# Attention slots one step later, two splits earlier, and two sets of decayed keys on GpSimd

## The chip, the cores and the metric

The kernel runs on one core of one Trainium2 chip. The metric is the device time of one execution in microseconds (us). The engines are TensorE (PE; its weight loads are shown apart as PEld), VectorE (DVE), ScalarE (ACT), GpSimd (POOL) and SyncE (SP, which here only issues DMAs).

## The reference, cut to what matters

Retention attention with a decay `lam` for each of 8 heads (2 batches, 768 positions, 64 columns a head) gives x, 1536 tokens by 512. Then two layers follow:

```python
# attention, block by block of the sequence
intra = (q k^T * Dmask) v ; inter = (q * lam_pow) kv_state
kv_state = lam_block * kv_state + (k * rev_pow)^T v      # "decayed keys" k * rev_pow
x   = attention as [1536, 512]
r   = np.maximum(x @ w_in, 0.0); x = (r * r) @ w_out     # layer 1, 512 -> 2048 -> 512
out = (1 / (1 + np.exp(-(x @ w_gate))) * (x @ w_val)) @ w_out   # layer 2, 512 -> 1536 -> 512
```

## The kernel before, in words

Everything is FP32 in value, computed on PE from two parts: each operand is split into a high part (`whi`, `xh`, `gh`) and a low part (`wlo`, `xl`, `gl`), and a product takes three groups of matmuls. A unit of layer 1's weights arrives over SP's queue as `raw` (512 KB). ACT takes it apart in two instructions (`scale_words`: `j`, `r`), DVE joins these (`join_words`: a shift and an add), the joined words are stored to DRAM (`w<-j`, 256 KB for a unit) and split: `whi` on ACT (on DVE for the first units), `wlo` on DVE, which needs `whi`. The stores free the buffers that later `j` and `r` reuse: `unit` hands out 27 buffers of 128x512 in turn, `double` 27 of 128x1024.

**Attention.** Twelve chunks of 128 positions are worked on in six pairs, (0, 6) to (5, 11). The first two pairs stand at the start. The other four are interleaved with layer 1's first block of 512 tokens ("block 0"). For a pair k there are two *scores* slots (`att_scores` on PE, a mask on DVE, a decayed query `qd` on POOL by `query`, decayed keys `kd` by `att_keys`) and one *out* slot (`att_uv`, `att_out` on PE, then the state on POOL and DVE). The table `SLOTS` says at which half step each stands, `LOADS` at which half step its q/k and k/v chunks and two pairs of weight units are asked for. `att_keys` of chunks 2 and 8 runs on ACT, eight instructions of 128x64; all others are one instruction of 128x512 on POOL.

**Block 0.** `step_1(f)` runs for f = 0 to 15; its half steps are 2f and 2f + 1. In order: A(f) (`stage_a`, through `mm_in`, 12 matmuls of a weight unit with x0 into one bank), the slot of half step 2f, `elem` and `split_g` on A(f)'s result (ACT `r`, `g`, `gh`, DVE `gl`), B(f-1) (`stage_b`, `mm_out`, 12 matmuls), the slot of half step 2f + 1, and then what `PLAN[f]` lists: `A` takes the next couple of raw units apart (`couple_act`, two ACT instructions a unit), joins them on DVE and asks for the next loads; `S` splits the oldest joined couple (`couple_split`). An `S` that leads the list is done ahead of B(f-1). The instructions stand on every engine in the order in which this program writes them; an engine works through them in that order.

**After block 0** the other 1024 tokens pass layer 1 by Strassen products (`block`, L733). Their operands are prepared at places of a clock that counts the planned matmul time (`at`, `passed`): `combine_x(1, places)` makes 11 combined operands `xch`/`xcl` (L616, L619) and differences `t` (L632), `combine_a` the weights' sums `as`, `ah`, `al`. `T1` is the planned time at which the Strassen products begin. `snap` (L742) and `evacuate` (L583) copy PSUM banks out on ACT, which frees them.

Of the kernel before, what the change touches and what calls it, by code (L numbers as in the profile page):

```python
# [9 lines left out]
AF = mybir.ActivationFunctionType  # L10
# [6 lines left out]
FILL = 8  # L17
SINGLE = 10
BY_DVE = 7
KEYS_BY_ACT = (2, 8)  # L20
PLAN = {
    0: "ASAS", 1: "ASAS", 2: "AAS", 3: "SAA", 4: "SAS", 5: "SAA", 7: "SAA", 9: "SAA",
    10: "SAS", 11: "SS", 12: "S", 13: "", 14: "", 15: "",
}

PAIRS = ((0, 6), (1, 7), (2, 8), (3, 9), (4, 10), (5, 11))
LEAD = 2
SLOTS = {
    7: ("scores", 2), 8: ("scores", 8), 10: ("out", 2),
    11: ("scores", 3), 12: ("scores", 9), 14: ("out", 3),  # L30
    15: ("scores", 4), 16: ("scores", 10), 18: ("out", 4),
    19: ("scores", 5), 20: ("scores", 11), 22: ("out", 5),
}
LOADS = {
# [3 lines left out]
}  # L38

MM = 0.2267  # L40
# [5 lines left out]
def retention_moe_kernel(  # L46
# [24 lines left out]
    nc = tc.nc  # L71
    NCH = qk.shape[0]
    NT = out.shape[2]
    SEQ_CH = NCH // 2
    H = lam.shape[0]
# [38 lines left out]
    qk_t, kv_t = {}, {}  # L114
# [143 lines left out]
    def run(ops):  # L258
        weave(ops, [])
# [4 lines left out]
    W = const.tile([P, H, 1], F32, name="W")  # L264
# [98 lines left out]
    def heads(t):  # L363
        return t.rearrange("s (h d) -> s h d", h=H)
# [11 lines left out]
    def query(i, eng=nc.gpsimd):  # L376
        b = slice(0, 64 if i == NCH else P)
        qd = qd_t[i] = unit("qd")
        eng.tensor_tensor(
            out=pv(qd)[b], in0=pv(qk_t[i][:, 0, :])[b], in1=L[b, i // (SEQ_CH + 1)],  # L380
            op=ALU.mult,
        )

    def att_keys(c, eng=nc.gpsimd):
        if c % SEQ_CH < SEQ_CH - 1:
            kd = kd_t[c] = unit("kd")
            if c in KEYS_BY_ACT:
                for h in range(H):
                    nc.scalar.activation(
                        heads(kd)[:, h], heads(kv_t[c][:, 0, :])[:, h], AF.Copy, scale=W[:, h]  # L390
                    )
                return
            eng.tensor_tensor(
                out=heads(kd), in0=heads(kv_t[c][:, 0, :]), in1=W.to_broadcast([P, H, 64]),
                op=ALU.mult,
            )

    def att_mask(c):
        s = c // SEQ_CH
        sc = sc_t.pop(c)  # L400
        at_t[c] = double("at")
        return [
            lambda g=g: nc.vector.tensor_tensor(
                out=pv(at_t[c][:, g, :]), in0=pv(sc[g]), in1=D[:, g ^ s], op=ALU.mult
            )
            for g in range(2)
        ]
# [108 lines left out]
            split_t[ph, f, u] = (hi, lo)  # L516
        return ops

    def mm_in(acc, w):
        (wh, wl), (xh, xl) = w, x0  # L520
        i = 0
        for a, b in ((wh, xh), (wl, xh), (wh, xl)):
            for kk in range(4):
                nc.tensor.matmul(  # L524
                    acc, lhsT=a[:, kk * P : (kk + 1) * P], rhs=b[:, kk, :],
                    start=i == 0, stop=i == 11,
                )
                i += 1
        passed(12 * MM)
# [14 lines left out]
    def stage_a(ph, f):  # L544
        accs = []
        for u in range(ph):
            accs.append(bank())
            mm_in(accs[u], split_t.pop((ph, f, u)))
        return accs

    def elem(ph, f, acc):
# [596 lines left out]
    def attend(half):  # L1148
        load(LOADS.get(half, ""))
        what, k = SLOTS.get(half, (None, 0))  # L1150
        if what == "scores":
            att_scores(k)
            passed(SCORES)

            def after():
                run(att_mask(k))
                att_keys(k)
                query(k if k < SEQ_CH else k + 1)
                qk_t.pop(k)

            return after
        if what == "out":
            pair = PAIRS[k]
            if k < SEQ_CH - 1:
                decayed()
            att_uv(pair)
            att_out(pair)
            for c in pair:
                kv_t.pop(c)
            passed(REST)  # L1170

            def after():
                att_state()
                att_x(pair)

            return after
        return lambda: None
# [57 lines left out]
    with tc.manual_schedule():  # L1235
        load_lam()
        load("q6", nc.scalar)
        load("q0 q7 v0 v6 w q1 q8 v1 v7 w w w w w")
        rows = decays()
        warm_up(WARM)  # L1240
        new_xr()
        first, second = PAIRS[:LEAD]
        for c in first:
            att_scores(c)
        warm_up(FILL)
        query(7)
        for c in first:
            att_keys(c)
        run([op for c in first for op in att_mask(c)])
        rows()  # L1250
        att_out(first)
        att_uv(first)
        j_0, r_0 = couple_ops()
        j_0()
        x_1 = att_x(first, r_0)
        run(couple_dve())
        att_state()
        for c in (1, 8):
            query(c)
        for c in second:  # L1260
            att_scores(c)
        lo_0 = couple_split()
        run([op for c in second for op in att_mask(c)])
        run(lo_0)
        run(x_1)
        for c in second:
            att_keys(c)
        decay_of_state()
        decayed()
        att_out(second)  # L1270
        run(att_x(second))
        for _ in range(2):
            couple_act()
            run(couple_dve())
            run(couple_split())
        att_uv(second)
        for c in (0, 6, 1, 7):
            qk_t.pop(c)
        for c in (0, 6, 1, 7):
            kv_t.pop(c)  # L1280
        clock[0] = 0.0
        flush()


        keys = [(1, i, 0) for i in range(NF1 // 2)]
        prepare_a(keys[0], T1 - 20.0)
        at(T1 - 20.0, lambda: load_a((1, 1, 0)))
        combine_x(1, [T1 + d for d in (-24, -22.5, -20.5, -18.5, -16, -13.5, -11, -8.5, -6, -3.5, -1)])
        for f in range(NF1):
            step_1(f)  # L1290
        n_out = 24
        for k in range(3):
            at(T2 - 14.0 + k, lambda: load_w(1))
        for k in range(n_out):
            convert(T2 + 1.0 + k * (T3 - T2 - 4.0) / n_out)
        for f in range(NF1):
            prepare_out(1, f, T2 + 24 * MM * f)
        uses = [use for i in range(NF1 // 2) for use in pair_in_1(i)]
        strassen(keys, uses, (None, lambda: close(1)))
        xc.clear()  # L1300
        new_xr()
        for f in range(2):
            at(T3 - 24.0 + f, lambda f=f: load_units(2, f))
        at(T3 - 14.0, lambda: run(split_w(2, 0)))
        pair_out(1)


        for f in range(2, NF2):
            at(T3 + (36 * (f - 1) - 12) * MM - 8.0, lambda f=f: load_units(2, f))
        for k in range(3 * NF2 - n_out):  # L1310
            convert(T3 + 2.0 + 3.6 * k)
        for i in range(NF2 // 2):
            sum_out_w(i, T4 - 64.0 + 9.0 * i)
        keys = [(2, i, u) for i in range(NF2 // 2) for u in range(2)]
        prepare_a(keys[0], T4)
        at(T4 - 28.0, lambda: combine_a((2, 0, 1)))
        at(T4 - 20.0, lambda: load_a((2, 0, 1)))
        combine_x(2, [T4 - 46.0 + 3.5 * k for k in range(11)])
        for f in range(NF2):
            step_2(f)  # L1320
        T6 = T5 + 6 * STEP
        by_unit_through_dram(1, T5 - 14.0, T5 - 7.0)
        through_dram(2, T5 - 4.0, T5 + 1.5)
        through_dram(3, T5 + 1.0, T5 + 6.5)
        through_dram(4, T5 + 6.0, T5 + 11.5)
        for n, load, pos in (
            (0, -21.0, -13.0), (1, -12.0, -1.5), (2, -6.0, 4.0),
            (3, 1.0, 8.8), (4, 6.0, 13.5), (5, 11.0, 18.3),
        ):
            prepare_w(0, n, n, T5 + load, T5 + pos)  # L1330
        for n, i, load, pos in (
            (0, 5, -12.5, -5.0), (1, 4, -7.5, -1.0), (2, 3, -3.0, 3.5),
            (3, 0, 1.0, 8.0), (4, 2, 6.0, 10.0), (5, 1, 10.0, 11.6),
        ):
            prepare_w(1, n, i, T6 + load, T6 + pos)
        by_unit_through_dram(2, T6 - 7.0, T6 + 5.0)
        by_unit_through_dram(1, T6, T6 + 10.2)
        uses = [use for i in range(NF2 // 2) for use in pair_in_2(i)]
        strassen(keys, uses, (None, lambda: close(2)))
        blocks_out()  # L1340
        flush()
        assert not agenda and not to_conv and not ready
# [62 lines left out]
```

## Time and profile before

| | |
|---|---|
| runs | 580.08, 581.56, 581.89 us; median 581.56 |
| profiled execution | 582.65 us, of it a span of 580.9 us that the trace shows |
| TensorE's granted clock over the span | 0.997 of 2.4 GHz |
| busy | PE 98%, DVE 77%, ACT 60%, POOL 10% |
| DMA | 150.25 MB, 259 GB/s on average |

A time in a timeline counts from the span's start. "[2.89 <-ACT whi L246]" behind a row is the idle time of that engine just before it and the work that ended it. Rows of one kind that follow each other stand as one row with their count (x4); its duration is that of the whole row.

### The profile page before, as it was taken

How to read it: one execution, taken by the hardware profiler on the slowest of the kernel's cores; microseconds unless marked ns; L12 is line 12 of the kernel's file. 1: busy time of each engine (PE TensorE's matmuls, PEld its weight loads, DVE VectorE, ACT ScalarE, POOL GpSimd, SP SyncE). 2: the span in 40 equal slices, each digit the busy share in tenths (PEclk: the TensorE clock that was granted, in tenths of full speed). 3: DMA queues.
4: the chain of work that ended last, by engine and by line, in shares of the span. 5: the costliest groups of instructions: out<-in, count | busy, mean ns of one | idle time of the engine just before them, and what ended most of it. 6: DMA issues, size and time to landing. Idle time of an engine off the chain costs nothing.

```text
span 580.9 us, 8565 instructions
## 1 busy us (share of the span) xinstructions
PE 569.4 (98%) x3018; PEld 463.4 (80%) x3018; DVE 448.1 (77%) x650; ACT 349.6 (60%) x562; POOL 55.9 (10%) x50
## 2 busy tenths in 40 slices
PE   8998999999999999999999999999999999999997
PEld 5876888888888888888888888888878888878785
DVE  7997877986788866776656778884778877779956
ACT  4678878857565557775648565534564555385452
POOL 6332351000000000000000000120102210000000
PEclk9998999999999999999999999999999999999999
DMA  8999998401454588999985899984447678588681
GB/s 309 407 408 413 343 365 292 139 18 63 129 182 151 177 313 320 410 410 412 401 335 179 292 352 343 367 254 91 139 113 207 199 198 234 166 314 312 195 321 72
DMA packets 69226, 150.25 MB, mean 259 GB/s; under 512 B 6976, under 2 KB 15168, under 8 KB 69184
## 3 DMA queue, kind: packets, MB, share of 16 engines
q1 hardware_dynamic: 65312, 144.86, 68.4%
q0 software_dynamic: 3360, 3.93, 4.5%
q10 hardware_dynamic: 512, 0.92, 0.5%
q8 instruction: 23, 0.38, 0.3%
q14 instruction: 19, 0.16, 0.1%
HBM read 105.91 MB, written 42.21 MB: 255 GB/s over the span
## 4 chain that ended last, share of the span: by engine, by line
PE 78%; DVE 7%; DMA 6%; ACT 4%; issue 2%; POOL 2%; DVEq 0%; SPq 0%; ACTq 0%; POOLq 0%
PE p L733 28%; PE p L524 17%; PE p L1124 15%; PE p L538 12%; DMA gr<-gs 2%; PE p L1053 2%; PE p L457 2%; PE p L371 1%; DMA gs<-gs 1%; DMA D<-wt 1%; DVE wq L1010 1%; DMA out_t<-c 1%; PE p L445 1%; DVE j L181 1%; DVE gs L868 1%
## 5 line engine op out<-in xcount | busy, mean ns | idle before, releaser
L733 PE MATMUL p<-xch,ah 128*128 128x512 f32 x280 | 110.0, 393 | 1.0 <-ACT s L742 0.5
L733 PE MATMUL p<-xch,al 128*128 128x512 f32 x280 | 109.1, 390 | 0.0
L733 PE MATMUL p<-xcl,ah 128*128 128x512 f32 x280 | 109.1, 390 | 0.0
L733 PEld LDWEIGHTS p<-xch,ah 128*128 128x128 f32 x280 | 52.6, 188 | 14.9 <-ACT s L742 3.2
L742 ACT COPY s<-p 128x512 f32<-128x512 f32 x60 | 35.1, 588 | 43.6 <-PE p L733 43.3
L733 PEld LDWEIGHTS p<-xch,al 128*128 128x128 f32 x280 | 52.6, 188 | 11.0
L733 PEld LDWEIGHTS p<-xcl,ah 128*128 128x128 f32 x280 | 52.6, 188 | 10.6
L747 DVE TENSOR_TENSOR c<-p,s 128x512 f32<-128x512 f32 x60 | 41.3, 688 | 23.0 <-PE p L733 23.0
L1053 PE MATMUL p<-gq,wq 128*128 128x512 f32 x252 | 58.0, 391 | 0.3 <-DVE wq L1010 0.2
L1053 PEld LDWEIGHTS p<-gq,wq 128*128 128x128 f32 x252 | 47.1, 188 | 11.1 <-DVE wq L1010 1.4
L181 DVE CUSTOM_DVE_ANT_0 j<-j,r 128x1024 uint16<-128x1024 uint16 (+1 forms) x57 | 48.5, 851 | 6.6 <-DVE j L176 0.5
L165 ACT ACTIVATE j<-raw 128x512 f32<-128x512 f32 x68 | 45.4, 668 | 10.1 <-DMA raw<-in_w 5.7
L1124 PE MATMUL p<-g2h,whi 128*128 128x512 f32 x128 | 49.8, 389 | 0.0
L1124 PE MATMUL p<-g2h,wlo 128*128 128x512 f32 x128 | 49.8, 389 | 0.0
L1124 PE MATMUL p<-g2l,whi 128*128 128x512 f32 x128 | 49.8, 389 | 0.0
L169 ACT ACTIVATE r<-raw 128x512 int32<-128x512 uint32 x68 | 45.0, 662 | 4.2 <-DMA w<-j 2.7
L524 PE MATMUL p<-xh,whi 128*128 128x512 f32 x160 | 44.5, 400 | 2.9 <-ACT whi L246 2.9
L524 PE MATMUL p<-xh,wlo 128*128 128x512 f32 x160 | 43.6, 395 | 1.3 <-DVE wlo L249 1.3
L524 PE MATMUL p<-xl,whi 128*128 128x512 f32 x160 | 42.8, 390 | 0.0
L681 POOL DMA_DIRECT2D as<-w x6 | 5.6, 926 | 354.9 <-DVE g L560 282.2
L524 PEld LDWEIGHTS p<-xh,whi 128*128 128x128 f32 x160 | 30.1, 191 | 9.8 <-ACT whi L246 3.3
L524 PEld LDWEIGHTS p<-xh,wlo 128*128 128x128 f32 x160 | 30.5, 191 | 8.3 <-DVE wlo L249 1.8
(128 smaller groups left out, 1029.0 us busy)
## 6 DMA issues: line engine op xcount, KB each, us to landing
raw<-in_w SPq DMA_DIRECT2D x68, 512.0 KB, 7.6
w<-j SPq DMA_DIRECT2D x68, 256.0 KB, 7.6
u<-w SPq DMA_DIRECT2D x52, 256.0 KB, 5.3
a<-w SPq DMA_DIRECT2D x20, 512.0 KB, 4.1
g<-g SPq DMA_DIRECT2D x32, 256.0 KB, 3.8
g<-g SPq DMA_DIRECT2D x16, 512.0 KB, 7.6
kv<-in_kv SPq DMA_DIRECT2D x12, 512.0 KB, 7.8
gr<-gs SPq DMA_DIRECT2D x24, 256.0 KB, 6.0
```

The source lines that it names most:

```text
L165: lambda: nc.scalar.activation(j, t[:, :, 1].bitcast(F32), AF.Prelu, scale=2.0**-80 if flip else 2.0**-112, alpha=2.0**-32 if flip else 2. ...
L169: lambda: nc.scalar.activation(r, low, AF.Copy, scale=2.0**-29),
L181: nc.vector.tensor_tensor(out=j, in0=j, in1=r, op=ALU.add)
L371: nc.tensor.matmul(pv(sc[g])[:, p, :], lhsT=pv(t[:, 1, :])[half(g), p, :], rhs=pv(t[:, 0, :])[half(g), p, :], start=True, stop=True,)
L457: nc.tensor.matmul(ov[s][half(r), p, :], lhsT=v[:, 2 * p + r, :], rhs=pv(at[:, r ^ s, :])[:, p, :], start=n == 0 and p == 0, stop=p == 3, ...
L524: nc.tensor.matmul(acc, lhsT=a[:, kk * P : (kk + 1) * P], rhs=b[:, kk, :], start=i == 0, stop=i == 11,)
L538: nc.tensor.matmul(acc[e], lhsT=a[:, e * P : (e + 1) * P], rhs=b, start=first and i == 0, stop=last and i == 2,)
L733: nc.tensor.matmul(acc, lhsT=w[:, col, kk * P : (kk + 1) * P], rhs=x[:, kk, :], start=start and i == 0, stop=stop and i == 5, skip_group_c ...
L742: nc.scalar.copy(s, acc)
L747: nc.vector.tensor_tensor(out=c, in0=acc, in1=s, op=ALU.add)
L1053: nc.tensor.matmul(acc[k], lhsT=a[:, wn], rhs=block_of(b, gn), start=first and n == 0, stop=last and n == 3 * len(group) - 1,)
L1124: nc.tensor.matmul(acc[e, t], lhsT=a[:, e * P : (e + 1) * P], rhs=b[:, t, :], start=first and i == 0, stop=last and i == 2,)
```

## The change

1. `SLOTS`: every slot stands two half steps, one step, later. `LOADS`: their loads one or two half steps later.
2. `PLAN`: steps 2, 3 and 4 change from `AAS`, `SAA`, `SAS` to `ASA`, `SAS`, `AAS`.
3. `KEYS_BY_ACT` is gone: the decayed keys of chunks 2 and 8 are one POOL instruction each.
4. `attend`: query and keys of a scores slot are issued directly behind its matmuls, the query first; only the mask stays behind the step's other work.
5. `mm_in` for f > 1: the group with `xl` comes second and the one with `wlo` last.
6. `combine_x(1)`: its 11 places lie between T1 - 16 and T1 - 1 instead of T1 - 24 and T1 - 1.

```diff
-KEYS_BY_ACT = (2, 8)
 PLAN = {
-    0: "ASAS", 1: "ASAS", 2: "AAS", 3: "SAA", 4: "SAS", 5: "SAA", 7: "SAA", 9: "SAA",
+    0: "ASAS", 1: "ASAS", 2: "ASA", 3: "SAS", 4: "AAS", 5: "SAA", 7: "SAA", 9: "SAA",
...
 SLOTS = {
-    7: ("scores", 2), 8: ("scores", 8), 10: ("out", 2),
...
-    19: ("scores", 5), 20: ("scores", 11), 22: ("out", 5),
+    9: ("scores", 2), 10: ("scores", 8), 12: ("out", 2),
...
+    21: ("scores", 5), 22: ("scores", 11), 24: ("out", 5),
 }
 LOADS = {
-    2: "q2", 3: "q9", 4: "v2", 5: "v8",
+    3: "q2", 4: "q9", 6: "v2", 7: "v8",
...
     def att_keys(c, eng=nc.gpsimd):
...
-            if c in KEYS_BY_ACT:
-                for h in range(H):
-                    nc.scalar.activation(
-                        heads(kd)[:, h], heads(kv_t[c][:, 0, :])[:, h], AF.Copy, scale=W[:, h]
-                    )
-                return
...
-        for a, b in ((wh, xh), (wl, xh), (wh, xl)):
+        for a, b in ((wh, xh), (wh, xl), (wl, xh)) if late else ((wh, xh), (wl, xh), (wh, xl)):
...
-                mm_in(accs[u], split_t.pop((ph, f, u)))
+                mm_in(accs[u], split_t.pop((ph, f, u)), f > 1)
...
-            def after():
-                run(att_mask(k))
-                att_keys(k)
-                query(k if k < SEQ_CH else k + 1)
-                qk_t.pop(k)
-
-            return after
+            query(k if k < SEQ_CH else k + 1)
+            att_keys(k)
+            qk_t.pop(k)
+            return lambda: run(att_mask(k))
...
-        combine_x(1, [T1 + d for d in (-24, -22.5, -20.5, -18.5, -16, -13.5, -11, -8.5, -6, -3.5, -1)])
+        combine_x(1, [T1 + d for d in (-16, -15, -13.5, -12, -10.5, -9, -7.5, -6, -4.5, -3, -1)])
```

Lines of the changed kernel stand 1 to 11 lower than before (L246 becomes L245, L524 L517, L555 L548, L619 L612, L632 L625, L697 L690, L742 L735).

ACT, from `whi` of A(5)'s weights (`whi_674`, after the change `whi_587`) to the `whi` of the couple that holds B(4)'s weights (`whi_706`, after the change `whi_669`). Before:

```order
L165 ACTIVATE j_591<-raw 128x512
L169 ACTIVATE r_592<-raw 128x512
L389 ACTIVATE kd<-kv,W 128x64 x8
L165 ACTIVATE j_613<-raw 128x512
...
L568 CAST gh<-g 128x512
L389 ACTIVATE kd<-kv,W 128x64 x8
L246 CAST whi_674<-j_591 128x512
L165 ACTIVATE j_694<-raw 128x512
...
L169 ACTIVATE r_695<-raw 128x512
L246 CAST whi_706<-j_613 128x1024
```

And after the change:

```order
L164 ACTIVATE j_579<-raw 128x512
L168 ACTIVATE r_580<-raw 128x512
L245 CAST whi_587<-j_579 128x512
L548 ACTIVATE r<-p 128x512
L549 ACTIVATE g<-r 128x512
L561 CAST gh<-g 128x512
L164 ACTIVATE j_642<-raw 128x512
...
L168 ACTIVATE r_658<-raw 128x512
L245 CAST whi_669<-j_642 128x1024
```

The row of `whi` for A(5) now follows its own `j` and `r` directly; between the two `whi` rows there are now `r`, `g`, `gh` and eight instructions that take raw units apart (`j_642`, `r_643` twice and `j_657`, `r_658` twice), where there were four (`j_694`, `r_695` twice).

POOL, behind the state of the first pairs (`tt`); the rows are those of chunks 2 and 8. Before:

```order
L411 TENSOR_TENSOR tt<-S,G 128x512
L379 TENSOR_TENSOR qd<-qk,L 128x512 x2
L411 TENSOR_TENSOR tt<-S,G 128x512
L393 TENSOR_TENSOR kd<-kv,W 128x512
L379 TENSOR_TENSOR qd<-qk,L 128x512
```

And after the change:

```order
L404 TENSOR_TENSOR tt<-S,G 128x512
L378 TENSOR_TENSOR qd<-qk,L 128x512
L386 TENSOR_TENSOR kd<-kv,W 128x512
L378 TENSOR_TENSOR qd<-qk,L 128x512
L386 TENSOR_TENSOR kd<-kv,W 128x512
L404 TENSOR_TENSOR tt<-S,G 128x512
```

Two `kd` are added there, one behind each `qd`.

DVE, the last rows ahead of the first weights' sums `as` of the Strassen part, from the `gl` of step 14 on. Before:

```order
L570 TENSOR_TENSOR gl_1546<-g_1542,gh_1545 128x512
L619 TENSOR_TENSOR xcl_1539<-t_1522,xch_1538 128x1024
L619 TENSOR_TENSOR xcl_1563<-xr_158,xch_1562 128x1024
L632 TENSOR_TENSOR t_1579<-xr_158,t_1479 128x1024
L570 TENSOR_TENSOR gl_1586<-g_1582,gh_1585 128x512
L619 TENSOR_TENSOR xcl_1602<-t_1579,xch_1601 128x1024
L697 TENSOR_TENSOR as_1617<-a_1451 128x256
```

And after the change:

```order
L563 TENSOR_TENSOR gl_1525<-g_1521,gh_1524 128x512
L625 TENSOR_TENSOR t_1540<-xr_158 128x1024
L612 TENSOR_TENSOR xcl_1514<-t_1498,xch_1513 128x1024
L612 TENSOR_TENSOR xcl_1518<-xr_158,xch_1517 128x1024
L612 TENSOR_TENSOR xcl_1545<-t_1540,xch_1544 128x1024
L625 TENSOR_TENSOR t_1564<-xr_158,t_1498 128x1024
L563 TENSOR_TENSOR gl_1571<-g_1567,gh_1570 128x512
L612 TENSOR_TENSOR xcl_1561<-xr_158,xch_1560 128x1024
L612 TENSOR_TENSOR xcl_1588<-t_1564,xch_1587 128x1024
L690 TENSOR_TENSOR as_1603<-a_1428 128x256
```

Between the `gl` of step 14 and `as` there are three rows of 128x1024 more than before: seven beside the two `gl`, where there were four.

## Rows read from the trace of the kernel before

**Rows 1.** Windows: busy time of the engines, granted clock, DMA share, GB/s.

```profile
core 0: us, PE busy (x) PEld busy (x) DVE busy (x) ACT busy (x) POOL busy (x), PEclk, DMA share, GB/s
20.00:58.00 38.00, 33.77 (x207) 26.63 (x206) 33.27 (x49) 31.25 (x63) 8.14 (x6) 0.96 1.03 410
58.00:130.00 72.00, 72.00 (x635) 58.46 (x626) 59.30 (x66) 54.96 (x85) 15.35 (x10) 1.00 0.65 232
```

**Rows 2.** Timeline of PE: start, duration (us), line, out<-in, idle before.

```profile
43.17 1.19 PE L524 MATMUL p<-xh,wlo 128*128 128x512 f32 x4 [1.34 <-DVE wlo L249]
...
52.21 2.08 PE L524 MATMUL p<-xh,whi 128*128 128x512 f32 x4 [2.89 <-ACT whi L246]
...
56.61 1.15 PE L429 MATMUL p<-kv,kd 128*64 128x64 f32 x32
```

**Rows 3.** Timeline of ACT.

```profile
37.83 0.66 ACT L169 ACTIVATE r<-raw 128x512 int32<-128x512 uint32 x1 [2.70 <-DMA w<-j]
...
42.54 0.67 ACT L165 ACTIVATE j<-raw 128x512 f32<-128x512 f32 x1
...
43.67 2.01 ACT L389 ACTIVATE kd<-kv,W 128x64 f32<-128x64 f32 x8
...
47.81 0.60 ACT L555 ACTIVATE r<-p 128x512 f32<-128x512 f32 x1
...
49.64 2.01 ACT L389 ACTIVATE kd<-kv,W 128x64 f32<-128x64 f32 x8
51.56 0.60 ACT L246 CAST whi<-j 128x512 fp32r<-128x512 f32 x1
...
54.34 1.03 ACT L246 CAST whi<-j 128x1024 fp32r<-128x1024 f32 x1
```

**Rows 4.** Windows around PE's longest wait.

```profile
43.00:48.00 5.00, 4.83 (x31) 3.82 (x32) 4.14 (x8) 5.00 (x15) 0.00 (x0) 1.00 1.02 407
52.00:54.00 2.00, 1.79 (x4) 1.49 (x5) 0.80 (x2) 2.00 (x5) 0.00 (x0) 0.50 1.03 421
```

**Rows 5.** Timelines of DVE and POOL.

```profile
37.30 1.53 DVE L176 TENSOR_SCALAR j<-j 128x512 int32<-128x512 int32 x1
...
39.57 0.42 DVE L176 TENSOR_SCALAR j<-j 128x512 int32<-128x512 int32 x1
...
36.98 1.56 POOL L379 TENSOR_TENSOR qd<-qk,L 128x512 f32<-128x512 f32 x1 [16.60 <-PE p L524]
...
63.14 1.04 POOL L411 TENSOR_TENSOR tt<-S,G 128x512 f32<-128x512 f32 x1 [1.77 <-DVE S L471]
```

**Rows 6.** Timeline of PE, beginning of the Strassen part.

```profile
137.48 0.39 PE L733 MATMUL p<-xch,ah 128*128 128x512 f32 x1
...
144.28 0.39 PE L733 MATMUL p<-xch,ah 128*128 128x512 f32 x1
...
145.64 0.39 PE L733 MATMUL p<-xch,ah 128*128 128x512 f32 x1
```

**Rows 7.** Timeline of DVE there.

```profile
132.99 0.69 DVE L570 TENSOR_TENSOR gl<-g,gh 128x512 fp32r<-128x512 f32 x1 [1.79 <-ACT gh L568]
133.60 1.22 DVE L619 TENSOR_TENSOR xcl<-t,xch 128x1024 fp32r<-128x1024 f32 x1
134.74 1.22 DVE L619 TENSOR_TENSOR xcl<-xr,xch 128x1024 fp32r<-128x1024 f32 x1
...
139.35 0.42 DVE L697 TENSOR_TENSOR as<-a 128x256 f32<-128x256 f32 x1
...
140.48 0.43 DVE L700 TENSOR_TENSOR as<-a,as 128x256 f32<-128x256 f32 x1
```

**Rows 8.** Timeline of ACT there.

```profile
140.94 1.05 ACT L706 CAST ah<-as 128x1024 fp32r<-128x1024 f32 x1 [1.30 <-DVE as L700]
...
142.37 2.05 ACT L583 COPY xd<-p 128x512 f32<-128x512 f32 x4
144.48 0.59 ACT L742 COPY s<-p 128x512 f32<-128x512 f32 x1
```

More of the change, by code (lines that the diff above doesn't have):

```diff
@@ L28 @@
 SLOTS = {
-    7: ("scores", 2), 8: ("scores", 8), 10: ("out", 2),
-    11: ("scores", 3), 12: ("scores", 9), 14: ("out", 3),
-    15: ("scores", 4), 16: ("scores", 10), 18: ("out", 4),
-    19: ("scores", 5), 20: ("scores", 11), 22: ("out", 5),
+    9: ("scores", 2), 10: ("scores", 8), 12: ("out", 2),
+    13: ("scores", 3), 14: ("scores", 9), 16: ("out", 3),
+    17: ("scores", 4), 18: ("scores", 10), 20: ("out", 4),
+    21: ("scores", 5), 22: ("scores", 11), 24: ("out", 5),
 }
 LOADS = {
[3 rows of a table removed]
[3 rows of a table added]
 }
@@ L517, in split_w, with mm_in @@
         return ops
-    def mm_in(acc, w):
+    def mm_in(acc, w, late):
         (wh, wl), (xh, xl) = w, x0
         i = 0
-        for a, b in ((wh, xh), (wl, xh), (wh, xl)):
+        for a, b in ((wh, xh), (wh, xl), (wl, xh)) if late else ((wh, xh), (wl, xh), (wh, xl)):
             for kk in range(4):
```

4 rows, old and new, of the table LOADS are left out of this document.

## The prediction

> **What bounds the kernel now.** I read the windows first. PE is busy for 72.00 of the 72 us from 58 to 130, and for 33.77 of the 38 us from 20 to 58 [rows 1]. So the slots of pairs 3 to 5 lie where PE never waits, and moving them can win nothing; only 20 to 58 holds something to win. There the timeline of PE shows two waits: 1.34 us for DVE's `wlo` ahead of A(4)'s second group, and 2.89 us for ACT's `whi` ahead of A(5). After the second, A(5) takes 56.61 - 52.21 = 4.40 us [rows 2]. Twelve such matmuls take 2.72 us in the Strassen part (36 of them from 137.48 to 145.64 [rows 6]), so 1.68 us more are lost: the granted clock was 1.00 from 43 to 48 and 0.50, its 1.2 GHz level, from 52 to 54, behind the wait [rows 4]. All that can be recovered is 1.34 + 2.89 + 1.68 = 5.9 us.
>
> Why `whi` was late is in ACT's timeline. ACT never pauses from 43 to 48 [rows 4]. A(5)'s `j` is read at 42.54, but its `whi` comes at 51.56, behind two sets of decayed keys of 2.01 us each, four conversions, and `r`, `g`, `gh` [rows 3]. The wait for `wlo` has another root: ACT stood for 2.70 us until 37.83 for the store `w<-j` that frees a buffer [rows 3], and DVE then took 1.53 us for a shift beside POOL's `qd`, where the next one took 0.42 [rows 5].
>
> **The change, part by part.** *Keys on GpSimd, and the split of A(5) moved up.* Both take work from between A(5)'s `j` and its `whi`: 4.0 us of keys, and the other couples' conversions. What ACT is spared is work it must partly do later, which is the point of the next part. On POOL a `kd` is one 128x512 product with a broadcast operand. Its bound below is the 1.04 us of `tt` alone, above the 1.56 us of `qd` that had DVE beside it [rows 5]; I take 1.04 and count the overlap on DVE apart.
>
> *DVE beside POOL.* [rows 5] show that a shift of 0.42 us took 1.53, that is 1.11 longer, while POOL's `qd` ran. The Trainium skill ("SBUF — State Buffer", section "SBUF: two separate sides") says that the two share a port pair which one instruction holds to its end while the other blocks; it speaks against keys on GpSimd. The trace agrees, the excess being about one POOL instruction; no excess would be counted without it.
>
> *A(4).* The first store stood behind one more 512 KB load than now. At 407 GB/s [rows 4] that load is 1.29 us, so the store lands at about 36.5 instead of 37.8, and ACT reads A(4)'s raw unit 1.3 us earlier. DVE's shift and add follow to about 38.5 (the `qd` now comes behind the add), `whi` ends at 39.2 and `wlo` at 40.3. A(4) needs the first at 39.5 and, since `wlo` is now its last group, the second at 41.3. I count the 1.34 us as gone. B(3)'s `whi` ends at about 42.6, where PE wants it at 42.2; scores and B(3) bring PE to A(5) at 46.5.
>
> *A(5).* Its `j` and `r` run until 43.7 as before. POOL's `kd` of chunk 2 needs a k/v chunk which lands behind the first store, two more stores of 0.64 (half a load), two loads, two stores and itself: 36.5 + 6.4 = 42.9. Then DVE's shift and add meet `kd` and `qd`. If both block, the add ends at 46.5, otherwise at 44.7; I take 46.5, and `whi` at 47.2. PE waits 0.7 us for A(5), not 2.89, and reaches B(4) behind scores of chunk 8 at about 51.3.
>
> *B(4), what is late next.* The order on ACT is `r`, `g`, `gh` (47.81 to 49.64 before, 1.83 us [rows 3]), then eight conversions where four stood, then `whi` of B(4). A conversion is (43.67 - 42.54)/2 = 0.57 us [rows 3], so 47.1 + 1.83 + 8 x 0.57 = 53.4, and `whi` (1.03 us [rows 3]) ends at 54.4. PE wants it at 51.3: **a new wait of 3.1 us at B(4)**. It is as long as that of before, and I expect the low clock after it again, 1.68 us. B(4) ends at 54.4 + 2.72 + 1.68 = 58.8, and its `wlo`, behind two masks and near POOL's second `kd`, can delay its second group by 0.3 to 0.9: 59.1 to 59.7, say 59.4. The kernel before has not done B(4) at that place: it stands at 56.61 behind A(5) [rows 2], and with B(4)'s 2.72 it would be at 59.33. The sum of the first part is **+0.1 us**. Bounds: without the low clock and the late `wlo` B(4) ends at 57.1, -2.2; if POOL and DVE don't meet at A(5) either, `whi` is 1.8 earlier and B(4) could end at 55.3 to 56.0, -3.3 to -4; with every delay +1.
>
> The Trainium skill ("TensorE: Matmul & The Clock Gate", section "Why this matters for your kernels") advises against idle gaps between bursts, since the clock then drops. The trace agrees by the 0.50 of [rows 4]; the rule would add the same 1.68 us.
>
> *Slots and loads one step later* cost nothing for pairs 3 to 5 as long as PE stays busy: ACT is busy 54.96 and DVE 59.30 of 72 us there [rows 1], a step of slack either way. If that cover is gone, one late `whi` costs 0.6 to 1.
>
> *`combine_x` squeezed.* The last out slot is one step later, so x for the Strassen part is complete later, and DVE does more at the end. Let T be the first Strassen matmul, 137.48 before [rows 6]. The `gl` of step 14 starts at 132.99, T - 4.5, and is released by ACT's `gh`, which follows A(14) on PE [rows 6, 7]; that stays. Behind it stand now seven rows of 128x1024 and one more `gl` ahead of `as`. Rows follow each other at 134.74 - 133.60 = 1.14, `gl` takes 133.60 - 132.99 = 0.61 [rows 7]: 7 x 1.14 + 2 x 0.61 = 9.2 us. So `as` starts at T + 4.7, where before it started at 139.35, T + 1.9. Its four rows take 140.91 - 139.35 = 1.56 [rows 7], so it ends at T + 6.2. On ACT `ah` (about 1 us) waits for `as`, and behind it, in order, stand the copy `s`, four copies `xd` of 2.05 in sum, and the second `s` [rows 8]. Each `s` frees a PSUM bank for a block of PE. From the end of `as` to the end of the second `s` passed 145.07 - 140.91 = 4.16 us [rows 7, 8]; so it ends at T + 10.3. The block that needs it began at 145.64, T + 8.16 [rows 6], having had 0.57 us of reserve. **A new wait of 2.1 us**, of which 0.9 falls already to the block at T + 6.8 (144.28 [rows 6]), whose bank the first `s` frees at T + 7.7. Bounds: the seven rows can start before `gl` where ACT is done earlier (up to one and a half rows, 1.5 us less: +0.6), or one row more falls behind it (+0.4: +2.5). Nothing behind gives this back: PE is the bound and all later blocks shift.
>
> *The order in `mm_in`* is the same number of matmuls; it only gives `wlo` 0.9 us more, counted above.
>
> **Sum.** +0.1 + 2.1 = +2.2 us on the profiled execution's 582.65, which lies 1.1 above the median of the runs. On the median: 581.56 + 2.2 = **583.8 us**. Faster or slower than 0.3%, 1.74 us, is about what a measurement of this kernel can tell from no change.
>
> **The rivals.**
>
> *A: as worked out*, with own range +1.0 to +3.2 (582.6 to 584.8). Chance 0.45; 0.28 of it lies over 1.74.
>
> *B: the first part wins about what the second costs.* The low clock stays away at B(4), or DVE meets only one of POOL's two instructions at A(5): -2.2 + 2.1 = -0.1, 581.5 us. For it: `whi` at A(5) needs just one of the two overlaps to be missed. Against: the wait at B(4) is as long as the one that lowered the clock before. Chance 0.25, nearly all the same.
>
> *C: faster.* The Strassen wait stays at 0.6, since DVE does the rows ahead of step 14's `gl` where it is idle 1.79 us [rows 7], and B(4) ends at 56 to 57, so -3.3 + 0.6 = -2.7: 578.9 us. It decides where B(4)'s `whi` ends before 52.5, that is where the add for A(5) ends before 45. Chance 0.20, of which 0.16 is faster.
>
> *D: slower than A.* A second scores slot collides: the conversions of step 5 (`SAA`) now meet the state of pair 2 and its masks, and A(7) or B(6) waits like B(4), 1 to 2 us more: 585.3 us. Against it: ACT and DVE have room from 58 on [rows 1]. Chance 0.10.
>
> That the change does nothing is B by another way: the places in the order are different, so it isn't a rival of its own.
>
> **How the numbers follow.** The time is A's, 583.8. The range goes from 580.0 (C's upper half) to 585.4 (D's middle); left out are most of C, about 0.13, and half of D, 0.05. Faster: 0.16 of C and 0.01 of B, 0.17. Slower: 0.28 of A and D's 0.10, 0.38. The same: 0.45.
>
> **What would show it.** A(4) runs without an idle time ahead of its `wlo`. A(5)'s wait for `whi` is under 1 us. B(4) waits about 3 us for ACT's `whi`, L245, and the granted clock falls to about a half behind it. ACT runs eight conversions in a row ahead of that `whi`. From the end of B(4) on no wait until the Strassen part, whose first `as` starts 4.7 us behind the first Strassen matmul, and two blocks at L726 wait for ACT's `s` by 0.9 and 1.2 us. Wrong would be the first part if B(4)'s `whi` comes within 1 us of its need, and the second if `as` starts before T + 3.

## The result, and the profile after

| | before | changed |
|---|---|---|
| median of 6 runs | 581.63 us (580.08 to 582.20) | 585.22 us (584.39 to 586.83) |
| ratio, with its 95% interval | | 1.0061 [1.0044, 1.0078] |
| profiled execution: own time, span | 582.65, 580.9 | 584.39, 582.3 |
| start of the Strassen part | 137.48 | 137.68 |
| start of the last phase (L1053, now L1046) | 518.71 | 521.09 |

The change is slower, by 3.6 us in the medians. Its 585.22 us lies inside the range of the forecast, 1.4 us over the number. First the timeline of PE of the changed kernel, the part that answers to [rows 2] (start, duration, line, out<-in, idle before):

```profile
41.18 1.07 PE L517 MATMUL p<-xh,wlo 128*128 128x512 f32 x4
42.70 1.19 PE L531 MATMUL p<-gh,whi 128*128 128x512 f32 x4 [0.45 <-ACT whi L245]
...
47.03 1.20 PE L517 MATMUL p<-xh,whi 128*128 128x512 f32 x4 [0.23 <-ACT whi L245]
...
51.14 1.16 PE L370 MATMUL p<-qk 64*128 64x128 f32 x14 [0.66 <-DVE at L396]
54.77 2.01 PE L531 MATMUL p<-gh,whi 128*128 128x512 f32 x4 [2.48 <-ACT whi L245]
56.80 1.87 PE L531 MATMUL p<-gh,wlo 128*128 128x512 f32 x4
...
59.42 1.07 PE L517 MATMUL p<-xh,whi 128*128 128x512 f32 x4
```

The two waits of before are gone: no idle time ahead of A(4)'s `wlo` at 41.18, and 0.23 us at A(5). In their place PE waits 2.48 us at B(4), and before that 0.66 us at the scores of chunk 8, which need banks that DVE's mask of chunk 2 frees. B(4) ends at 59.42. The windows of the changed kernel show the clock there (columns as in [rows 1], PEclk third from the end):

```profile
54.00:58.00 4.00, 3.21 (x7) 2.11 (x8) 3.86 (x6) 3.94 (x7) 0.47 (x1) 0.61 1.03 417
58.00:60.00 2.00, 2.00 (x10) 1.61 (x9) 2.00 (x2) 2.00 (x5) 2.00 (x2) 0.93 1.03 410
```

The clock falls behind the wait, as in [rows 4]. Why `whi` is late is in the timelines of ACT, of DVE and of POOL, which follow in this order:

```profile
36.56 0.68 ACT L164 ACTIVATE j<-raw 128x512 f32<-128x512 f32 x1 [3.38 <-DMA w<-j]
...
46.36 0.62 ACT L245 CAST whi<-j 128x512 fp32r<-128x512 f32 x1 [2.58 <-DVE j L180]
...
52.62 0.65 ACT L168 ACTIVATE r<-raw 128x512 int32<-128x512 uint32 x1
53.67 1.05 ACT L245 CAST whi<-j 128x1024 fp32r<-128x1024 f32 x1 [0.40 <-DVE j L180]
```

```profile
43.37 1.27 DVE L175 TENSOR_SCALAR j<-j 128x512 int32<-128x512 int32 x1
44.77 1.56 DVE L180 CUSTOM_DVE_ANT_0 j<-j,r 128x1024 uint16<-128x1024 uint16 x1
...
48.82 1.66 DVE L563 TENSOR_TENSOR gl<-g,gh 128x512 fp32r<-128x512 f32 x1 [1.04 <-ACT gh L561]
50.41 1.27 DVE L396 TENSOR_TENSOR at<-p,D 128x512 f32<-128x512 f32 x2
51.61 0.68 DVE L175 TENSOR_SCALAR j<-j 128x1024 int32<-128x1024 int32 x1
52.42 1.22 DVE L180 CUSTOM_DVE_ANT_0 j<-j,r 128x2048 uint16<-128x2048 uint16 x1
```

```profile
42.95 1.40 POOL L386 TENSOR_TENSOR kd<-kv,W 128x512 f32<-128x512 f32 x1 [2.99 <-DMA kv<-in_kv]
44.31 1.47 POOL L378 TENSOR_TENSOR qd<-qk,L 128x512 f32<-128x512 f32 x1
...
48.64 1.29 POOL L378 TENSOR_TENSOR qd<-qk,L 128x512 f32<-128x512 f32 x1
```

Each DVE row that lies beside a POOL row takes 0.85 to 0.97 us longer than alone (the shift 0.42 in [rows 5], `gl` 0.69 in [rows 7], the add 0.69 at 37.83 of this trace); shift and add together lose 1.7 us ahead of A(5)'s `whi`, for which ACT stands still for 2.58 us. Ahead of B(4)'s `whi` ACT is ready at 53.27 (its last conversion), but DVE's add of that couple ends at 53.64: ACT waits the last 0.40 us for DVE. Now the Strassen part, PE, then DVE, then ACT, to be read beside [rows 6] to [rows 8]; the last fence is PE of the kernel before, for the start of its last phase:

```profile
137.68 0.39 PE L726 MATMUL p<-xch,ah 128*128 128x512 f32 x1
...
145.39 0.50 PE L726 MATMUL p<-xch,ah 128*128 128x512 f32 x1 [0.75 <-ACT s L735]
...
147.83 0.50 PE L726 MATMUL p<-xch,ah 128*128 128x512 f32 x1 [0.78 <-ACT s L735]
...
521.09 0.61 PE L1046 MATMUL p<-gq,wq 128*128 128x512 f32 x2
```

```profile
133.07 0.69 DVE L563 TENSOR_TENSOR gl<-g,gh 128x512 fp32r<-128x512 f32 x1 [2.74 <-ACT gh L561]
...
142.23 0.41 DVE L690 TENSOR_TENSOR as<-a 128x256 f32<-128x256 f32 x1
```

```profile
147.15 0.63 ACT L735 COPY s<-p 128x512 f32<-128x512 f32 x1
```

```profile
518.71 0.62 PE L1053 MATMUL p<-gq,wq 128*128 128x512 f32 x2
```

With T = 137.68, `as` starts at T + 4.55 and the block that began at T + 8.16 before begins at T + 10.15: 1.99 us later. So the two traces stand 0.20 us apart at T, 2.19 behind the two waits and 2.38 at the last phase. That the spans differ by only 1.4 is the last phase's doing, which took 58.34 us in the profiled execution of before (to its last matmul at 577.05) and 57.41 in this one.

### The profile page after: what moved, and what is told of

It is laid out like the page before. It is cut to its first block, busy times and chain, and to the rows that moved or that the text cites. A ratio compares the mean times of both kernels' runs of the same rounds, so it can differ in the third digit from the quotient of the medians.

```text
span 582.3 us, 8547 instructions
## 1 busy us (share of the span) xinstructions
PE 570.0 (98%) x3018; PEld 463.1 (80%) x3018; DVE 446.7 (77%) x650; ACT 344.8 (59%) x546; POOL 53.0 (9%) x52
## 4 chain that ended last, share of the span: by engine, by line
PE 81%; DMA 6%; DVE 6%; ACT 5%; issue 2%; DVEq 0%; SPq 0%; ACTq 0%
PE p L726 27%; PE p L517 15%; PE p L1117 15%; PE p L531 10%; PE p L1046 10%; DMA raw<-in_w 2%; DMA kv<-in_kv 2%; DMA w<-j 2%; PE p L450 1%; PE p L370 1%; DVE xcl L612 1%; DVE c L740 1%; ACT ah L699 1%; ACT s L735 1%; DMA qk<-in_qk 1%
## 5 line engine op out<-in xcount | busy, mean ns | idle before, releaser
L735 ACT COPY s<-p 128x512 f32<-128x512 f32 x60 | 35.1, 588 | 43.5 <-PE p L726 43.4
L1046 PE MATMUL p<-gq,wq 128*128 128x512 f32 x252 | 57.4, 389 | 0.0
L1046 PEld LDWEIGHTS p<-gq,wq 128*128 128x128 f32 x252 | 47.2, 188 | 10.1 <-DVE wq L1003 0.2
L517 PE MATMUL p<-xh,whi 128*128 128x512 f32 x160 | 43.5, 394 | 0.2 <-ACT whi L245 0.2
L517 PE MATMUL p<-xl,whi 128*128 128x512 f32 x160 | 42.8, 389 | 0.0
L517 PE MATMUL p<-xh,wlo 128*128 128x512 f32 x160 | 42.8, 389 | 0.0
L563 DVE TENSOR_TENSOR gl<-g,gh 128x512 fp32r<-128x512 f32 x28 | 21.9, 782 | 19.1 <-ACT gh L561 19.1
L531 PE MATMUL p<-gh,whi 128*128 128x512 f32 x112 | 32.9, 407 | 2.9 <-ACT whi L245 2.9
```

Source lines behind the costliest of these rows:

```text
L517: nc.tensor.matmul(acc, lhsT=a[:, kk * P : (kk + 1) * P], rhs=b[:, kk, :], start=i == 0, stop=i == 11,)
L531: nc.tensor.matmul(acc[e], lhsT=a[:, e * P : (e + 1) * P], rhs=b, start=first and i == 0, stop=last and i == 2,)
L563: lambda: nc.vector.tensor_tensor(out=gl, in0=src, in1=gh, op=ALU.subtract)
L735: nc.scalar.copy(s, acc)
L1046: nc.tensor.matmul(acc[k], lhsT=a[:, wn], rhs=block_of(b, gn), start=first and n == 0, stop=last and n == 3 * len(group) - 1,)
```

## The experiments

Each was timed beside the kernel before, so the median of before differs a little from one comparison to the next.

**1. The squeeze alone.** In the kernel before:

```diff
-combine_x(1, [T1 + d for d in (-24, -22.5, ..., -3.5, -1)])
+combine_x(1, [T1 + d for d in (-16, -15, -13.5, -12, -10.5, -9, -7.5, -6, -4.5, -3, -1)])
```

> The kernel before with only the 11 places of combine_x squeezed to T1 - 16 to T1 - 1; slots, plan, keys and mm_in as before. My theory (the squeezed rows on DVE make the weights' sums late, and ACT's copies that free PSUM banks late with them): the first 'as' starts about 4.6 us behind the first Strassen matmul instead of 1.9, PE waits for ACT's s at two blocks, the Strassen blocks come 1.5 to 2.0 us later, and the time is 1.5 to 2.2 us over the kernel before: 583.1 to 583.8. Rival (the squeeze costs only because the last out slot is a step later, so that DVE meets both): as starts under T + 3, no wait, the same time as before.

Measured: 583.57 against 581.87 us, ratio 1.0028 [1.0014, 1.0042]. PE of this kernel:

```profile
144.88 0.50 PE L733 MATMUL p<-xch,ah 128*128 128x512 f32 x1 [0.75 <-ACT s L742]
...
147.31 0.50 PE L733 MATMUL p<-xch,ah 128*128 128x512 f32 x1 [0.78 <-ACT s L742]
```

The same two waits to the hundredth, with the slots where they were. From the first Strassen matmul (137.16) to the last phase (520.54) it takes 2.15 us longer than before (381.23). The rival is out: the squeeze needs no later slot.

**2. The keys alone.** In the kernel before:

```diff
-KEYS_BY_ACT = (2, 8)
+KEYS_BY_ACT = ()
```

> The kernel before with only the keys of chunks 2 and 8 put on GpSimd. Theory 1 (ACT's 4 us of keys were what made A(5)'s whi late, and GpSimd's share of DVE costs little here): PE's wait of 2.9 us for whi and the low clock behind it go, 3.5 to 4.6 us less than before, 577.0 to 578.1. Theory 2 (DVE and GpSimd hold each other up, so that DVE's joins come late instead): DVE's shift and add of the couple ahead of A(5) or B(4) take 1.3 to 1.6 us each, whi or wlo are late by 1 to 3 us, and less than 2 us are won, 579.6 to 582.

Measured: 580.15 against 581.87, ratio 0.9965 [0.9952, 0.9979], a gain in the span of theory 2. PE, then DVE of this kernel:

```profile
44.22 1.77 PE L524 MATMUL p<-xh,wlo 128*128 128x512 f32 x4 [2.04 <-DVE wlo L249]
```

```profile
41.03 1.45 DVE L181 CUSTOM_DVE_ANT_0 j<-j,r 128x1024 uint16<-128x1024 uint16 x1
42.41 1.75 DVE L249 TENSOR_TENSOR wlo<-j,whi 128x512 fp32r<-128x512 f32 x1
```

The wait for `whi` of A(5) is gone, but A(4) waits longer for its `wlo`, which DVE does at 42.41, behind the next couple's join. Each of these rows has one of POOL's keys or queries beside it; alone they take some 0.7 us.

**3. B(4)'s couple taken apart and split earlier.** In the changed kernel:

```diff
-3: "SAS", 4: "AAS"
+3: "SAAS", 4: "SA"
```

> The changed kernel with PLAN 3 as SAAS instead of SAS and PLAN 4 as SA instead of AAS: B(4)'s weights are taken apart while ACT waits 2.6 us for DVE ahead of A(5)'s whi, and are split ahead of B(3)'s successor. Theory 1 (the place of B(4)'s couple in the order is what makes its whi late): PE's 2.5 us wait at B(4) and the low clock behind it (1.6 us) go, A(5) waits up to 0.5 us more; 3.3 to 4.2 us less than the changed kernel, 581.0 to 581.9. Theory 2 (DVE is the bound there, since it shares with GpSimd): the join of the second couple is late as well, B(4) still waits 1 us or more, less than 2 us are won.

Measured: 585.12, ratio to before 1.0051 [1.0033, 1.0068], the changed kernel's time. PE, then ACT, then DVE of this kernel:

```profile
50.45 1.19 PE L517 MATMUL p<-xh,wlo 128*128 128x512 f32 x4 [1.28 <-DVE wlo L248]
...
53.88 1.52 PE L370 MATMUL p<-qk 64*128 64x128 f32 x14 [1.81 <-DVE at L396]
55.33 2.07 PE L531 MATMUL p<-gh,whi 128*128 128x512 f32 x4
```

```profile
49.83 1.05 ACT L245 CAST whi<-j 128x1024 fp32r<-128x1024 f32 x1 [1.00 <-DVE j L180]
```

```profile
47.95 1.85 DVE L180 CUSTOM_DVE_ANT_0 j<-j,r 128x2048 uint16<-128x2048 uint16 x1
```

B(4)'s `whi` is 3.8 us earlier, and B(4) still starts at 55.33: the wait moved to A(5)'s `wlo` and to the scores of chunk 8. DVE has no idle time from 42.8 to 59, and the join took 1.85 us beside POOL, 1.22 alone. Theory 2 holds.

**4. The last combinations behind T1.** In the changed kernel:

```diff
-(-16, -15, -13.5, -12, -10.5, -9, -7.5, -6, -4.5, -3, -1)
+(-16, -15, -13.5, -12, -10.5, -9, -7.5, -6, 2, 4.5, 7)
```

> The changed kernel with the last three places of combine_x (B21, T4 and its split) behind T1, at T1 + 2, + 4.5 and + 7, and the others at the first eight places of the changed list. My theory: DVE reaches the first 'as' at about T + 1.2 instead of T + 4.6, both waits of PE for ACT's s (0.75 and 0.78 us) go, 1.5 to 2.0 us less than the changed kernel, 583.2 to 583.7. Rival (the operands that are made behind T1 are late in turn): PE waits for xcl of B21 or xch of T4 by 1 us or more, and the time stays at 585.

Measured: 584.96, ratio 1.0048 [1.0032, 1.0064]. Both waits for `s` are gone from the trace and nothing is late in their place; from the first Strassen matmul (138.50) to the last phase (520.31) it takes 381.81 us, 1.6 less than the changed kernel's 383.41. The time shows only 0.3 of it, and lies outside the span of the theory. All its runs had a mean clock of 0.993 or 0.994, and PE of its trace shows why:

```profile
54.73 2.07 PE L531 MATMUL p<-gh,whi 128*128 128x512 f32 x4 [2.48 <-ACT whi L245]
...
58.62 1.74 PE L531 MATMUL p<-gl,whi 128*128 128x512 f32 x4
60.20 1.08 PE L517 MATMUL p<-xh,whi 128*128 128x512 f32 x4
```

The wait at B(4) is the same 2.48 us, but here the low clock lasts through the third group as well (0.50 from 58 to 60, against 0.93 in the changed kernel), and A(6) starts at 60.20, 0.78 later. Experiments 5 and 11 take the clock out of the comparison.

**5. The gap filled.** In the changed kernel's `step_1`, ahead of B(f - 1):

```diff
+if f == 5:
+    warm_up(10)
```

> The changed kernel with ten matmuls on a constant tile (as in the warm-up, into a bank that nobody reads) between the scores of chunk 8 and B(4): PE has something to do for about 2 us of its 2.5 us wait. All products of the reference stay. Theory 1 (the low clock is brought on by the gap): the wait for ACT's whi stays, B(4) still starts at 54.7 us, but at full clock, and ends 1.6 to 3.2 us earlier than with a low stretch; the records' mean clock goes from 0.994 to 0.999 or 1.0, and the time is 1.6 to 3 us under the changed kernel, 582.2 to 583.6. Theory 2 (the clock falls for another reason, or the ten matmuls delay B(4) by what they save): 584.5 to 586, clock 0.994 to 0.997.

Measured: 584.28 (583.73 to 584.87), ratio 1.0046 [1.0028, 1.0064], and a mean clock of 0.998 to 1.0 in all five runs. PE of this kernel:

```profile
52.25 2.33 PE L334 MATMUL p<-warm 128*128 128x512 bf16 x10
54.80 1.20 PE L531 MATMUL p<-gh,whi 128*128 128x512 f32 x4 [0.22 <-ACT whi L245]
56.83 1.19 PE L531 MATMUL p<-gh,wlo 128*128 128x512 f32 x4 [0.82 <-DVE wlo L248]
...
58.78 1.07 PE L517 MATMUL p<-xh,whi 128*128 128x512 f32 x4
```

Here the gap brings the low clock on: filled, the clock is 1.00 from 50 to 59. But a wait for `wlo` of 0.82 us comes to light that the slow first group had covered, so B(4) ends 0.64 us earlier than in the changed kernel's trace, not 1.6: theory 1 has the cause, and the size is near theory 2's.

**6. Four conversions instead of eight.** In the changed kernel:

```diff
-4: "AAS"
+4: "ASA"
```

> The changed kernel with PLAN 4 as ASA instead of AAS: whi of B(4)'s couple stands behind four conversions on ACT instead of eight. Theory 1 (the conversions on ACT make B(4) late, as the prediction had it): whi about 2 us earlier, PE's wait at B(4) under 1 us, no low clock, 2.5 to 4 us less than the changed kernel, 581.2 to 582.7. Theory 2 (DVE is as late with the join of that couple: behind gl, the mask and GpSimd's instructions it ends at 53.6): whi at 53.6 as before, the wait still 2.4 us, same time as the changed kernel within 0.7 us.

Measured: 585.54, ratio 1.0066 [1.0047, 1.0084]. ACT, then DVE of this kernel:

```profile
53.85 1.04 ACT L245 CAST whi<-j 128x1024 fp32r<-128x1024 f32 x1 [2.63 <-DVE j L180]
```

```profile
52.60 1.23 DVE L180 CUSTOM_DVE_ANT_0 j<-j,r 128x2048 uint16<-128x2048 uint16 x1
```

ACT is now free 2.6 us earlier and spends them waiting for DVE's add. Theory 2: DVE is as late as ACT.

**7. Keys back on ACT.** The changed kernel with `KEYS_BY_ACT = (2, 8)` and its branch in `att_keys` again.

> The changed kernel with the keys of chunks 2 and 8 on ACT again, everything else as changed. Theory 1 (ACT's time ahead of B(4)'s whi is what counts): 2.0 us of keys stand between gh and the conversions, B(4)'s whi ends at 55.5 instead of 54.7, its wait is 0.7 to 2 us longer, 585.9 to 587.2. Theory 2 (DVE held up by GpSimd is what counts): without two of GpSimd's products DVE's joins are 1 to 2 us earlier, whi of A(5) and of B(4) as well, and the time is 0.5 to 1.5 us under the changed kernel.

Measured: 585.24, ratio 1.0064 [1.0046, 1.0083]: the changed kernel's time, and neither theory's number. PE of this kernel:

```profile
43.96 1.20 PE L538 MATMUL p<-gh,whi 128*128 128x512 f32 x4 [1.87 <-ACT whi L246]
...
55.66 1.71 PE L538 MATMUL p<-gh,whi 128*128 128x512 f32 x4 [3.53 <-ACT whi L246]
```

B(4) waits 1.05 us longer behind ACT's keys, as theory 1 has it. B(3) waits 1.87 instead of 0.45, because both `qd` and `tt` now follow each other on POOL from 38.52 to 42.70 and meet the join of B(3)'s weights. A(5) and the scores wait no more. In sum A(6) starts at 60.31, 0.89 later than in the changed kernel's trace; the medians don't show it.

**8. Parts 3, 4 and 5 without the later slots.** The changed kernel with `PLAN`, `SLOTS`, `LOADS` and the places of `combine_x` of the kernel before.

> Slots, loads, plan and combine_x's places as before, with parts 3, 4 and 5 of the change: keys of chunks 2 and 8 on GpSimd, query and keys issued right behind the scores, wlo's group last. Theory 1 (the later slots and the squeeze are what costs, the rest gains): as the kernel with the keys alone, whose wait of 2.0 us for wlo at A(4) shrinks by 0.9 us and perhaps loses its low clock: 578.0 to 579.5. Theory 2 (the rest brings nothing beyond the keys): 579.8 to 580.5.

Measured: 580.83, ratio 0.9986 [0.9973, 0.9999]. Theory 2 is nearer, and misses by 0.3. PE of this kernel:

```profile
47.38 1.16 PE L370 MATMUL p<-qk 64*128 64x128 f32 x14 [1.68 <-DVE at L396]
...
54.63 1.15 PE L422 MATMUL p<-kv,kd 128*64 128x64 f32 x32
```

**9. The same with the changed loads of pair 2.** In the kernel of experiment 8:

```diff
-2: "q2", 3: "q9", 4: "v2", 5: "v8",
-7: "q3",
+3: "q2", 4: "q9", 6: "v2",
+7: "v8 q3",
```

> As the kernel with parts 3, 4 and 5 alone, and the four loads of pair 2 one or two half steps later, as the change has them (slots as before). Theory 1 (the store that frees a buffer is what makes A(4) late, and GpSimd's instructions meet DVE's joins there): the store lands 1.3 us earlier, the keys come behind A(4)'s join, the 0.6 us wait at A(4) and most of the 1.7 us wait at the scores of chunk 8 go; 1 to 2 us under the kernel with parts 3, 4 and 5, 578.8 to 579.8. Theory 2 (GpSimd holds DVE up wherever its instructions stand): the waits move to A(5) or B(4), same time within 0.7 us, 580.1 to 581.5.

Measured: 581.06, ratio 0.9995 [0.9980, 1.0011]: theory 2. PE of this kernel:

```profile
53.48 1.20 PE L517 MATMUL p<-xh,wlo 128*128 128x512 f32 x4 [2.94 <-DVE wlo L248]
54.61 1.15 PE L422 MATMUL p<-kv,kd 128*64 128x64 f32 x32
```

A(4), its scores and B(3) run without a wait, and A(5) gives all of it back: the out slot starts at 54.61, in experiment 8 at 54.63. In both DVE's `wlo` of A(5) starts at 52.7 to 52.8, behind the join and the mask of other work. Behind this wait of 2.94 us the granted clock stayed at 1.00 (53.4 to 58): in this execution the gap did not bring the low clock.

**10. The gap filled in the kernel before.** In its `step_1`, ahead of A(f):

```diff
+if f == 5:
+    warm_up(11)
```

> The kernel before with eleven matmuls on a constant tile ahead of A(5), in its 2.9 us wait; all products of the reference stay. Theory 1 (the low clock comes from that gap, in most executions but not all, and costs 1.7 us where it comes): mean clock 1.0 in all runs, 580.2 to 580.6 in the median, 1.2 to 1.6 us under the kernel before, whose fastest runs it equals. Theory 2 (another wait shows up below the low stretch, such as that for wlo): clock 1.0, but less than 0.8 us won.

Measured: 580.99 against 581.18, ratio 0.9996 [0.9983, 1.0009]. All twelve runs had a clock of 0.999 or 1.0, so the gap is the cause here too. The gain is theory 2's, without the late `wlo` that it named: none shows in the trace. Part of the reason is the yardstick: of the 29 runs of before in this comparison 15 had 0.998 or more without a fill. The rest is open. In the trace the Strassen part starts at 135.91, 1.57 us earlier than before, yet the median lies 0.7 above that of before's runs at full clock (580.3, see below).

**11. Both mends.** Experiments 4 and 5 together.

> The changed kernel with both mends: the last three places of combine_x behind T1, and ten matmuls on a constant tile in the gap at B(4). Theory 1 (squeeze and low clock are separate costs that add up): 1.5 to 2.1 us under the kernel with the filled gap alone (584.3), 582.2 to 582.8, and still 0.3 to 1 us over the kernel before, since the waits of block 0 stay. Theory 2 (the late combos bring nothing in the time, as the 585.0 of the kernel with them alone seemed to say): 584 to 584.6.

Measured: 583.17, ratio 1.0034 [1.0019, 1.0048], 1.1 us under experiment 5. In the traces the last phase starts at 518.84 and 520.42: 1.58 us, all of it in the Strassen part, since both start that at 137.04. The costs add up, as theory 1 has it, but the time shows about 0.5 less than the trace and lies 0.4 above theory 1's span.

**12. A(5)'s split ahead of the next join.** In the kernel of experiment 9:

```diff
-3: "SAA", 4: "SAS"
+3: "SASA", 4: "SA"
```

> As the kernel with parts 3, 4 and 5 and the later loads of pair 2, with PLAN 3 as SASA instead of SAA and PLAN 4 as SA instead of SAS: A(5)'s weights are split before DVE joins the next couple (2.9 us of DVE with GpSimd beside it) and masks chunk 8. Theory 1 (PE's last wait of block 0, 2.9 us for wlo of A(5), comes from DVE's order): the wait goes, out of pair 2 starts near 51.7 us instead of 54.6, nothing else is late by more than 0.5 us, mean clock 1.0, 577.0 to 578.5. Theory 2 (DVE's work with GpSimd beside it is the bound of the stage, whatever the order): a new wait of 1.5 us or more for whi or wlo of B(4), and 579.3 to 581.

Measured: **578.21** us (577.05 to 578.67) against 581.67, ratio 0.9938 [0.9917, 0.9958]: faster than both kernels, theory 1. All runs had a clock of 0.999 or 1.0. PE of this kernel:

```profile
49.69 1.07 PE L517 MATMUL p<-xh,wlo 128*128 128x512 f32 x4
50.69 1.15 PE L422 MATMUL p<-kv,kd 128*64 128x64 f32 x32
...
55.73 1.20 PE L531 MATMUL p<-gh,whi 128*128 128x512 f32 x4
...
59.80 1.16 PE L370 MATMUL p<-qk 64*128 64x128 f32 x14 [0.64 <-ACT xr L476]
```

The out slot starts at 50.69 instead of 54.61, and B(4) follows it without a wait. The scores behind it wait 0.64 us for ACT's `xr`, a little more than the 0.5 that theory 1 allowed.

## Why the prediction was right, and where it was not

**A(4).** As forecast: the store landed at 36.5, A(4) started at 39.23 (39.5 forecast) and ran without a wait for `wlo`. B(3) waited 0.45 us for its `whi`, where 0.4 was forecast.

**A(5).** As forecast: POOL's `kd` started at 42.95, when its chunk had landed (42.9), DVE's shift met it, the add met `qd` and ended at 46.3 (46.5), and PE waited 0.23 us for `whi` (0.7). The Trainium skill ("SBUF — State Buffer", section "SBUF: two separate sides") has the two engines exclude each other for a whole instruction, where VectorE reads two operands from SBUF or runs in a mode that uses both of its ports. By that rule the excess is about one POOL product each time, and the rows above agree (0.85 to 0.97 us; `tt` alone took 1.04).

**B(4).** The place and the end were right: 59.42 for 59.4. Two steps on the way were not. The forecast named the eight conversions on ACT as what makes `whi` late; experiment 6 took four of them away and `whi` came no earlier, since DVE's add of that couple was equally late, behind `gl` beside POOL and a mask. And the 0.66 us at the scores of chunk 8 was not foreseen; it took a part of the wait that the forecast put at B(4), 2.48 for 3.1. That the end came out to 0.02 us is luck: B(4) started 0.37 us later than forecast and took 0.35 us less, as the next part shows.

**The low clock.** The term that was mis-sized in the first part is the sum of the low clock (1.68 us) and the late `wlo` (about 0.6): B(4) took 59.42 - 54.77 = 4.65 us where 5.0 was forecast. Experiment 5 shows that the gap brings the low clock on, and that the two don't add: at full clock PE waits 0.82 us for `wlo`, which the slow first group covers. So the low clock's own price was 0.64 us in this trace, and 60.20 - 58.78 = 1.4 us where it lasted longer (experiment 4). The Trainium skill ("TensorE: Matmul & The Clock Gate", section "Why this matters for your kernels") warns of idle gaps for this reason; experiments 5 and 10 agree that filling the gap keeps the clock up, and show that this alone won 0.9 us at most. Experiment 9 has a longer gap with no low clock behind it.

**What the low clock hides in the first part.** The forecast put the low clock at 1.68 us before and after, so that it dropped out of the +0.1. In the runs it took 1.57 and 0.64: with the gap filled the Strassen part starts at 135.91 in the kernel before (experiment 10) and at 137.04 in the changed kernel (experiment 5), earlier by as much than without. So at full clock block 0 of the changed kernel is 1.1 us longer, where the two traces show 0.20. Parts 3, 4 and 5 alone, whose trace is at full clock too, start it at 135.50 (experiment 8). What is left, 1.5 us, goes to the later slots and loads and the new `PLAN` together. No run has those alone: the 1.5 us is a difference of two traces.

**The Strassen part.** Forecast 2.1 us, measured 1.99 in the trace, with `as` at T + 4.55 for T + 4.7. Experiment 1 shows it alone (+1.7 us in the medians, 2.15 in the trace), experiments 4 and 11 take it away (1.6 us in the trace).

**The sum.** In the trace, 0.20 + 1.99 = 2.19 us where 2.2 was forecast. The medians differ by 3.6. That is the number of rival D (585.3) and over A's own range (584.8), but D's mechanism isn't in the trace: no later slot collides, PE is busy all the time from 58 to 130. The step that failed for the medians is another: the forecast compared one execution with one execution and carried the difference over to the median, leaving out how often each kernel falls into the low clock, a term put at nothing. Of the 80 runs of before beside the experiments, 26 had a mean clock of 0.9985 or more (median 580.3), 46 between 0.9945 and 0.9985 (581.85), 8 less (583.05). None of the changed kernel's 6 was in the first group: three had 0.996 or 0.997 (584.39 to 585.05), three 0.993 or 0.994 (585.40 to 586.83). Between runs of the same middle group the difference is 584.87 - 581.85 = 3.0; the rest to 3.6 is that half of the changed kernel's runs have the lower clock, and that a third of before's have the full one. Experiment 1, sorted in the same way, is 2.1 us over before in both of its groups, as its trace has it. Of the 3.0 the traces show 2.4 up to the last phase, and 0.3 lies outside the span that the trace shows: in the median of the runs the time is 1.78 us longer than the span before and 2.06 after. The other 0.3 stays open: the last phase took 57.3 to 58.5 us from one trace to the next, with both kinds of kernel at either end, and what a median run spends there isn't seen.

**Slots and loads a step later** cost nothing for pairs 3 to 5, as forecast: PE is busy 72.00 of the 72 us from 58 to 130 again.

## What to carry to other kernels

When a wait of the bound engine is traced to one feeder, look at what the other feeders would have been able to deliver: here ACT and DVE were equally late, so that four edits left the time: experiments 3, 7 and 9 moved the wait, and 6 left it where it was. The edit that paid (experiment 12) put one instruction of 0.7 us ahead of a join (3.6 us in experiment 9) that nobody waited for yet. And where work is moved to GpSimd, its time is also charged to VectorE, if both have work at that moment (the masks, which read PSUM, were not held up).

## What was not expected of the hardware

The same gap of PE, 2.48 us at B(4), was followed by a low clock of different length: in the changed kernel's trace to about 58.3 us, in experiment 4 through B(4)'s third group. Nor does the length of a wait alone decide whether it comes: behind 2.04 us it came (experiment 2, 0.50 from 46 to 48), behind 2.94 us it didn't (experiment 9). So it fits that 26 of the 80 runs of the kernel before had a mean clock of 0.9985 or more, although nothing fills its gap; that its gap was there in those runs is not shown, since none of them has a trace.

A shift with a single input on DVE (1.27 us at 43.37, 0.43 alone at 37.27 in the same trace) was held up by POOL as much as instructions with two inputs. Two masks that read PSUM were not: 1.28 us from 43.37 in experiment 9, beside POOL's `kd` (42.78 to 44.36), and 1.27 at 50.41 in the changed kernel, with POOL idle.
